# q of eight heads at a time by two 64-row PE tiles, with VectorE's steps queued by deadline

**Chip, cores, metric.** One core of one Trainium2 chip. The metric is device time in microseconds (us), the median of several executions of the whole program. PE is TensorE, ACT ScalarE, DVE VectorE, POOL GpSimd, SP SyncE.

## The reference, cut to what matters

```python
# S=2048 rows, D=576; 32 q heads, 16 k/v heads of 128; only the last W=512 keys are used
xn = layernorm(x)
q  = (xn @ wq)                      # 576 -> 32 heads x 128
p  = softmax(q @ k.T * Dh**-0.5)    # 512 keys, two q heads share one k/v head
s  = (p @ v) @ wo                   # 4096 -> 576
h  = gelu(layernorm(xn) @ w1)       # then rows shifted by -1, +1, -2, +2 per quarter
x1 = xn + shift(h) @ w2
g  = silu(x1 + gelu(layernorm(x1) @ w3) @ w4)
out = x + s * g
```

576 input rows are 4.5 chunks of the 128 rows that PE takes at once. That half chunk is what the change is about.

## The kernel before

Attention runs through 128 steps `u`: four blocks of 512 rows, 32 heads each. In a step PE makes the scores of a head (four matmuls of 512 columns, one ACT exp each), q of the next head (five matmuls) and the probabilities by v of the head before (16 matmuls of 129 columns). DVE divides by the row sum and writes a tile `o`, which a DMA transpose on the sync queue turns into `oT`. Matmuls of wo (block before), w1 and w2 are dealt out over the steps as filler. An MLP phase follows; it uses two 64-row tiles already.

```python
qT_pool = pool("qT_pool", 3)
o_pool = pool("o_pool", 4)          # four o tiles: four heads may wait for their transpose
...
def stage_q(u):
    qb, h = divmod(u, Hq)
    w = wq_b[(u // 4) % NWQ]
    hh = h % 4
    psq = ps_pq.tile([P, QB], FP32, name="psq", tag="pq")
    for kc in range(NDC):           # five chunks, the fifth half empty
        nc.tensor.matmul(psq[:, :], lhsT=w[:, kc, hh * Dh:(hh + 1) * Dh], rhs=xT_b[qb % 2][:, kc, :],
                         start=(kc == 0), stop=(kc == NDC - 1))
    ...                             # eviction to qT: DVE in block 0, ACT later
...
def stage_t(u):
    o = o_t.pop(u)
    oT = oT_pool.tile([P, TB, P], BF16, name="oT")
    last_t[0] = nc.sync.dma_start(out=oT[:], in_=o[:].rearrange("p a b -> p (a b)"), transpose=True)
...
at(2, lambda: late(pT_t[2][0][0:1, 0:1], load_w1))   # late: POOL waits for an exp, then issues the load
for i in range(8):
    at(4 + 3 * i, lambda i=i: late(pT_t[4 + 3 * i][0][0:1, 0:1], lambda: load_wo(i)))
...
for j in range(2, NB * 8):
    at(4 * (j - 1) - 1, lambda j=j: load_wq(j))      # wq for four heads at a time
...
for i in range(4):                                   # the main loop, one step u
    if u < U:
        stage_s(u, i)
    if i == 0:
        if u + 1 < U:
            stage_q(u + 1)                           # q follows the first score of every head
        for fn in fill.get(u, []):
            fn()
        continue
    if i < 3 and 0 <= u - 1 < U:
        stage_v(u - 1, 2 * (i - 1))
    for fn in cut[i - 1]:                            # filler, in thirds
        fn()
```

During the first 32 heads the POOL queue also loads nearly all of k, v, wo, w1 and the next x.

## Time and profile before

| | before |
|---|---|
| median of 3 runs | 851.1 us (850.77 to 858.88) |
| profiled span, mean granted clock | 847.5 us, 0.999 |
| first exp | 12.9 us |
| first exp to first exp, heads 0 to 31, 32 to 63, 64 to 95 | 103.1, 133.7, 134.3 us |
| heads 96 to 127, then to the MLP's first matmul | 137.4, 32.3 us |
| MLP | 293.7 us |

The phases are read from the trace's records of the exps and of the first MLP matmul. The first group of 32 is shorter because it carries no wo matmuls.

The prediction shows the page, the waits and one head. One view it did not use is that of the tile `oT`, the transposes of the attention output: duration of the issue (ns: min/median/max), who waited for the tile, and the time from issue to landing.

```profile
L395 SPq DMA_TRANSPOSE oT<-o x128: 1188/1192/2397, 18.4 to 523.9; - x128
  DVE o L387: 4.3, 2
DMA to landing us min/median/max: 2.4/3.2/9.8
```

DVE had twice waited, 4.3 us together, for an `o` tile to come free: the slowest transpose landed 9.8 us after its issue, and four tiles at one head per 2.88 us cover 11.5 us, of which filling a tile takes some. This queue was just long enough.

### The profile page before, as it was taken

The numbers are of one execution on the slowest core, as the hardware profiler recorded it, in microseconds if no ns is written. First come the engines' busy times: TensorE is split into PE (matmuls) and PEld (weight loads), VectorE is DVE, ScalarE is ACT, GpSimd is POOL, SyncE is SP. The second block draws the span as 40 slices with busy tenths as digits, with TensorE's granted clock in tenths as the row PEclk, the third lists the DMA queues.
The fourth block names the chain that finished last, engine by engine and source line by source line (L and its number), as shares of the span: only waits on it lengthen the run. The fifth ranks groups of instructions, "written<-read, shape, count | busy, mean of one in ns | idle before, by whom it ended". The sixth has DMA issues, their size and how long they took to land.

```text
span 847.5 us, 19375 instructions
## 1 busy us (share of the span) xinstructions
PE 826.8 (98%) x7896; PEld 485.0 (57%) x7980; DVE 427.7 (50%) x1351; ACT 460.9 (54%) x825; POOL 76.9 (9%) x134
## 2 busy tenths in 40 slices
PE   8999899999999999999999999999999999999996
PEld 5665555665564565565566565455555555555555
DVE  5778841267751166762154884052247537635324
ACT  5776763598793388784379874132333333334610
POOL 3441200310010111010001100000000000000000
PEclk9999999999999999999999999999999999999999
DMA  7996751473372174363048336992003301310101
GB/s 181 234 234 159 157 97 41 117 125 91 87 136 43 41 130 99 91 126 82 19 82 164 70 79 105 307 342 47 2 2 74 99 2 43 69 64 15 44 15 46
DMA packets 139983, 83.94 MB, mean 99 GB/s; under 512 B 106944, under 2 KB 133248, under 8 KB 139888
## 3 DMA queue, kind: packets, MB, share of 16 engines
q1 hardware_dynamic: 130048, 53.01, 30.6%
q0 software_dynamic: 8448, 28.15, 11.8%
q10 hardware_dynamic: 1392, 1.48, 0.5%
q8 instruction: 64, 1.05, 0.5%
q14 instruction: 31, 0.25, 0.1%
HBM read 49.17 MB, written 9.44 MB: 69 GB/s over the span
## 4 chain that ended last, share of the span: by engine, by line

## 5 line engine op out<-in xcount | busy, mean ns | idle before, releaser
L367 ACT ACTIVATE pT<-sc 128x512 bf16<-128x512 f32 x512 | 290.3, 596 | 103.5 <-PE sc L365 91.4
L365 PE MATMUL sc<-qT,kT 128*128 128x512 bf16 x493 | 175.1, 378 | 1.3 <-DVE qT L355 0.6
L382 PEld LDWEIGHTS <-pT 128*128 128x128 bf16 x2048 | 139.5, 98 | 52.9 <-DVE o L387 2.5
L382 PE MATMUL po<-v_sb,pT 128*128 128x129 bf16 x2048 | 161.4, 220 | 3.2 <-DVE o L387 2.0
L350 PE MATMUL psq<-xT_b,wq_b 128*128 128x512 bf16 x603 | 151.9, 379 | 2.5 <-DMA xT_b<-xn_b 0.4
L386 DVE RECIPROCAL ri_b<-po 128x2 f32<-128x2 f32 x256 | 43.0, 168 | 189.3 <-PE po L382 185.3
L731 PE MATMUL ph<-xT_b,w_s 64*128 64x512 bf16 x976 | 127.1, 376 | 2.3 <-DVE fence L721 2.1
L768 PE MATMUL pm<-w_s,h 64*128 64x512 bf16 x864 | 122.2, 377 | 0.9 <-DVE fence L721 0.9
L406 PE MATMUL pswo<-wo_sb,oT 128*128 128x512 bf16 x497 | 114.2, 379 | 0.8
L387 DVE TENSOR_TENSOR o<-po,ri_b 128x256 bf16<-128x256 f32 x256 | 107.9, 422 | 10.7 <-DMA oT<-o 4.3
L749 ACT ACTIVATE h<-ph 128x512 bf16<-128x512 f32 x67 | 39.4, 597 | 133.9 <-PE ph L731 133.9
L350 PEld LDWEIGHTS <-wq_b 128*128 128x128 bf16 x640 | 62.4, 98 | 74.4 <-issue 2.2
L768 PEld LDWEIGHTS <-h 64*128 64x128 bf16 x1728 | 70.8, 94 | 56.7 <-issue 1.6
L406 PEld LDWEIGHTS <-oT 128*128 128x128 bf16 x1024 | 64.9, 98 | 55.2
L768 PE MATMUL pr<-w_s,h 64*128 64x64 bf16 x864 | 90.2, 189 | 0.2 <-ACT h L749 0.2
L731 PEld LDWEIGHTS <-w_s 64*128 64x128 bf16 x1152 | 57.3, 94 | 51.0 <-issue 2.8
L357 ACT ACTIVATE qT<-psq 128x512 bf16<-128x512 f32 x96 | 57.4, 598 | 28.1 <-PE psq L350 26.7
L747 DVE COPY hx<-ph 128x512 f32<-128x512 f32 x55 | 38.0, 692 | 67.8 <-PE ph L731 67.8
L365 PEld LDWEIGHTS <-kT 128*128 128x128 bf16 x512 | 47.4, 97 | 28.4 <-DVE qT L355 1.2
L227 POOL DMA_DIRECT2D wq_b<-in_A_wq_dram x30 | 23.4, 780 | 314.4 <-PE psq L350 295.4
L721 DVE TENSOR_SCALAR fence<-ph,ph 1x1 f32<-1x1 f32 x61 | 12.6, 206 | 53.9 <-PE ph L731 53.4
L749 ACT ACTIVATE h<-hx 128x512 bf16<-128x512 f32 x55 | 34.6, 630 | 8.5 <-DVE hx L747 7.0
(114 smaller groups left out, 641.3 us busy)
## 6 DMA issues: line engine op xcount, KB each, us to landing
wq_b<-in_A_wq_dram POOLq DMA_DIRECT2D x30, 512.0 KB, 5.3
w_s<-in_B_w_dram SPq DMA_DIRECT2D x9, 576.0 KB, 7.0
wo_sb<-in_A_wo_dram POOLq DMA_DIRECT2D x8, 576.0 KB, 5.0
w_s<-in_B_w_dram SPq DMA_DIRECT2D x9, 512.0 KB, 7.9
x_dram<-x SPq DMA_DIRECT2D x4, 576.0 KB, 3.5
x<-x_dram SPq DMA_DIRECT2D x4, 576.0 KB, 5.1
s_b<-s_dram SPq DMA_DIRECT2D x4, 576.0 KB, 5.4
x_b<-in_A_x_dram SPq DMA_DIRECT2D x4, 576.0 KB, 6.6
```

What stands on the lines that cost most here:

```text
L350: nc.tensor.matmul(psq[:, :], lhsT=w[:, kc, hh * Dh:(hh + 1) * Dh], rhs=xT_b[qb % 2][:, kc, :], start=(kc == 0), stop=(kc == NDC - 1))
L357: nc.scalar.activation(out=qT[:, :], in_=psq[:, :], func=ACT.Copy)
L365: nc.tensor.matmul(sc[:, :], lhsT=kT[:, g, kc * P:(kc + 1) * P], rhs=qT_t[u][:, :], start=True, stop=True)
L367: nc.scalar.activation(out=pT[:, :], in_=sc[:, :], func=ACT.Exp, scale=SCALE)
L382: nc.tensor.matmul(po[:, j, :], lhsT=pTs[kc][:, tt * P:(tt + 1) * P], rhs=v_sb[:, g, kc, 0:Dh + 1], start=(kc == 0), stop=(kc == KCH - 1))
L386: nc.vector.reciprocal(out=ri, in_=po[:, :, Dh])
L387: nc.vector.tensor_tensor(out=o[:, t0:t0 + 2, :], in0=po[:, :, 0:Dh], in1=ri.unsqueeze(2).to_broadcast([P, 2, Dh]), op=ALU.mult)
L406: nc.tensor.matmul(ps, lhsT=oT_t[qb * Hq + h][:, tt, :], rhs=wo_sb[:, h, lo:hi], start=(h == 0), stop=(h == Hq - 1))
L731: nc.tensor.matmul(ps[i][:, :], lhsT=lhsT, rhs=xT[half, kc, :], start=first, stop=last, skip_group_check=True)
L747: nc.vector.tensor_copy(out=src[:, :], in_=ps[i][:, :])
L749: nc.scalar.activation(out=h3[:, :], in_=src[:, :], func=ACT.Gelu_apprx_tanh)
L768: nc.tensor.matmul(out, lhsT=h3_t[b, fc][half, tt * P:(tt + 1) * P], rhs=w4_s[fc // WS][half, fc % WS, lo:hi], start=key not in started, s ...
```

## The change

**Intent.** A half chunk of one head and a half chunk of another run side by side on two 64-row tiles of PE, so two heads take 9 slots in place of 10. As each change between 128-row and 64-row matmuls costs about 0.1 us (read from the trace in the prediction), q is made in blocks of eight heads. DVE and ACT get a fixed order, in which a small scheduler deals LN and gelu steps by deadline, against a credit that grows with PE's estimated time.

```diff
-        qT_pool = pool("qT_pool", 3)
-        o_pool = pool("o_pool", 4)
+        qT_pool = pool("qT_pool", 8)
+        o_pool = pool("o_pool", 5)
...
-            eng.dma_start(out=w[0:DR, NF, :], in_=A_wq[NF * P:D, c0:c0 + 4 * Dh])
+            for half in (LO, HI):                      # the tail of wq in both halves
+                eng.dma_start(out=w[half, NF, :], in_=A_wq[NF * P:D, c0:c0 + 4 * Dh])
...
-        def stage_q(u): ...
+        def stage_qs(u0, n):
+            unit(0.7)                                  # DVE: LN/gelu steps for up to 0.7 us
+            for u2 in range(u0, u0 + n, 4):
+                pairs = []
+                for u in (u2, u2 + 2):
+                    psp, tag = ((ps_pq, "pq"), (ps_po, "po"))[(u == u2) == (u0 > 0)]
+                    ps = [psp.tile([P, QB], FP32, name="psq", tag=tag) for _ in range(2)]
+                    q_half(xT, u, ps, [(kc, ((0, LO), (1, HI))) for kc in range(NDC)], True)
+                    f = small.tile([1, 1], FP32, name="fence")      # DVE reads both banks
+                    nc.vector.tensor_scalar(out=f[:, :], in0=ps[0][0:1, 0:1], scalar1=ps[1][0:1, 0:1],
+                                            scalar2=None, op0=ALU.add)
+                    unit(0.7)
+                    pairs.append((u, ps))
+                for u, ps in pairs:                    # then the halves swapped
+                    q_half(xT, u, ps, [(kc, ((1, LO), (0, HI))) for kc in range(NF)], False)
+                    ...
+                    nc.scalar.activation(out=qT_t[u][:, :], in_=ps[0][:, :], func=ACT.Copy)
+                    nc.vector.tensor_copy(out=qT_t[u + 1][:, :], in_=ps[1][:, :])
...
+        def pe(u, atoms, us=0.216):                    # filler, with its time for the credit
+            pe_fill.setdefault(u, []).extend((fn, us) for fn in atoms)
...
+                pe(u + 3, b2_rem(bb))                  # twenty 64-column matmuls, counted at 0.216
...
-        for j in range(2, NB * 8):
-            at(4 * (j - 1) - 1, lambda j=j: load_wq(j))
+        at(1, lambda: load_wq(2))
+        for j in range(3, NB * 8):                     # two at once
+            at(8 * (j // 2 - 1) + 1 + j % 2 if j > 3 else 4, lambda j=j: load_wq(j))
...
+                if u == 4:
+                    stage_qs(4, 4)
+                elif u % 8 == 0 and 0 < u < U:
+                    stage_qs(u, 8)
                 for i in range(4):
...
+                    v, tt = (u - 2, 2 + i) if i < 2 else (u - 1, i - 2)
+                    if 0 <= v < U:
+                        stage_v(v, tt)
+                    for fn, t in atoms[n * i // 4:n * (i + 1) // 4]:   # filler, in quarters
+                        fn()
+                    quarter(us)                        # credit for DVE steps
```

Filler tables, LN steps and buffers of x are moved to suit; the MLP gets finer LN steps.

## The prediction

> **What bounds the kernel now.** I read the page first: busy shares, then the slices.
>
> ```profile
> PE 826.8 (98%) x7896; PEld 485.0 (57%) x7980; DVE 427.7 (50%) x1351; ACT 460.9 (54%) x825; POOL 76.9 (9%) x134
> PE   8999899999999999999999999999999999999996
> ACT  5776763598793388784379874132333333334610
> PEclk9999999999999999999999999999999999999999
> ```
>
> TensorE (PE) is the candidate, at full clock. ScalarE (ACT) averages half, but its slices swing between 3 and 9: an average over stages with different limits. Attention, which the change touches, ends where the first matmul of the MLP starts, at 553.77 us (line below). The waits of PE inside 17 to 553.7 us:
>
> ```profile
> PE po L382 <- DVE o L387: 2.0, 1, 2.0
> PE psq L350 <- DMA xT_b<-xn_b: 0.4, 1, 0.4
> PE po L382 <- ACT pT L367: 0.3, 1, 0.3
> ```
>
> Only 2.7 us of 537. So PE itself bounds attention, and matmuls must be counted by start-to-start, not by their modelled durations. One plain head, from the timeline at 241.7 us (PE and ACT lines; L365 scores, L382 probabilities by v, L350 q, L367 exp, L357 the q eviction):
>
> ```profile
> 241.72 0.38 PE L365 MATMUL sc<-qT,kT 128*128 128x512 bf16 x1
> 241.92 0.60 ACT L357 ACTIVATE qT<-psq 128x512 bf16<-128x512 f32 x1 [0.21 <-PE psq L350]
> 241.94 0.63 PE L382 MATMUL po<-v_sb,pT 128*128 128x129 bf16 x8
> 242.41 0.38 PE L365 MATMUL sc<-qT,kT 128*128 128x512 bf16 x1
> 242.42 2.17 ACT L367 ACTIVATE pT<-sc 128x512 bf16<-128x512 f32 x4
> 242.62 0.63 PE L382 MATMUL po<-v_sb,pT 128*128 128x129 bf16 x8
> 243.09 0.59 PE L365 MATMUL sc<-qT,kT 128*128 128x512 bf16 x2
> 243.29 0.17 DVE L386 RECIPROCAL ri_b<-po 128x2 f32<-128x2 f32 x1
> 243.49 0.42 DVE L387 TENSOR_TENSOR o<-po,ri_b 128x256 bf16<-128x256 f32 x1
> 243.52 1.24 PE L350 MATMUL psq<-xT_b,wq_b 128*128 128x512 bf16 x5
> 244.60 0.38 PE L365 MATMUL sc<-qT,kT 128*128 128x512 bf16 x1
> ```
>
> The head takes 244.60 - 241.72 = 2.88 us. Five q matmuls take 244.60 - 243.52 = 1.08, so 0.2155 each; four scores 0.86; eight v matmuls 242.41 - 241.94 = 0.47, so 0.94 for sixteen, 0.0588 each. Sum 2.88: no gap. Over attention: 512 score, 640 q, 512 wo, 100 w1 and 80 w2 matmuls of 512 columns are 1844 x 0.2155 = 397; 2048 v by 0.0588 = 120; 592 of 64 columns at about 0.03 (81 wo remainders took 2.53 us) = 18; K transposes 3. That is 538 against 537 measured.
>
> Second reading: ACT. The q eviction starts at 241.92 and the next exp at 242.42, although its scores were ready before: 0.495 us per 128x512 tile back to back, less than the 0.596 duration. A head's four exps need 4 x 0.495 = 1.98 us, and with the eviction 2.47 of 2.88. PE hides that now.
>
> **What the Trainium skill says.** *TensorE: Matmul & The Clock Gate*, Part 1, "Wait - 56ns, not 53.3ns?": warm 512-column matmuls start 215.7 ns apart; the trace has 0.2155 us. *TensorEngine Tiling (Array Packing)*, "Key Properties": tiles work in parallel, but changing the tiling mode drains TensorE; and "Gotcha 1: PSUM Pressure": different row tiles must not access one PSUM bank at the same time, which is why each half pass is followed by a fence. *ScalarE: Activation LUTs*, "What ACT_TABLE_LOAD costs": 186 ns + 0.833 ns per column, overlapping by about 93 ns back to back, so an estimate of 0.52 us for 512 columns; the trace says 0.495, which I use.
>
> The MLP of this kernel already runs two 64-row tiles, so pairs and mode switches can be measured:
>
> ```profile
> 551.31 2.53 PE L406 MATMUL pswr<-wo_sb,oT 128*128 128x64 bf16 x81
> 553.77 1.04 PE L731 MATMUL ph<-xT_b,w_s 64*128 64x512 bf16 x8
> ...
> 574.92 1.04 PE L731 MATMUL ph<-xT_b,w_s 64*128 64x512 bf16 x8
> 575.78 0.40 PE L731 MATMUL ph<-xT_b,w3r_s 64*128 64x512 bf16 x2
> ...
> 804.45 1.04 PE L731 MATMUL ph<-xT_b,w_s 64*128 64x512 bf16 x8
> 805.42 1.58 PEld L931 LDWEIGHTS <-h 128*128 128x128 bf16 x14 [0.42 <-issue]
> ```
>
> Four pairs take 575.78 - 574.92 = 0.86, 0.215 a pair: two 64-row matmuls cost one slot. Switching back, the last pair started at about 805.10, so without a switch the next would start at 805.32; it starts at 805.43: 0.11 us. The switch in at 553.77 is also about 0.1 us late.
>
> **The change, part by part.**
>
> 1. *q.* 576 rows are 4.5 chunks of 128; before, a head takes 5 slots, the fifth half empty. Two heads by two tiles take 9 slots instead of 10. 64 pairs save 64 slots x 0.2155 = **-13.8 us**, all on PE. That is the whole direct gain, 1.6%.
>
> 2. *Mode switches.* q now comes in blocks: 4 heads at the start, 4 at head 4, then 8 at each of 15 places. 17 blocks x 2 x 0.11 = **+3.7 us**.
>
> 3. *Entry of a block.* After the first, a block's first pair writes the two po banks. One has just been filled by the v matmuls before it and must be evicted first. In the timeline the v group's last matmul starts at about 243.03 and VectorE (DVE) ends its multiplication at 243.91, while PE could go on at 243.09: 0.82 us. 16 entries would be 13.1 us. I have only the order in the source for it (another order moves the wait to the end of the block), so I take half: **+6.5 us**.
>
> 4. *Inside a block.* Eight heads are 36 slots, 7.76 us. DVE has four fences (0.2 each), four evictions (0.69 each) and up to five allowances of 0.7 for LN and gelu steps: 7.1 us. An allowance ahead of a fence or eviction that is due makes PE wait, chiefly where the second four heads want the banks of the first. Estimate 0.15 to 0.3 for each of 17: **+2 to 4 us**, taken as 2.5.
>
> 5. *Between blocks.* A head without q is 0.86 + 0.94 = 1.80 us of PE but 1.98 of ACT. **ACT becomes the bound of plain heads.** Three score banks let PE run ahead only about 1.5 us, so in a block of q ACT starves. Heads with wo (6.9 us each), w1 (1.08) or w2 (1.08) matmuls stay on PE: 0, 12, 9 and 13 of the four times 32 heads by the new table; in the first 32, 14 have K transposes of 0.24, which nearly balance it. So about 62 plain heads lose 0.18 = 11 us, less about 0.4 each time PE has built up a lead from a filled head (about ten times): 7. With the first quarter about 8; I take three quarters: **+6 us**.
>
> 6. *LN and gelu in DVE order.* They are moved, not removed. PE now loses only 2.7 us to waits in attention, one of 2.0 behind a q/k/v-side transfer; I credit **-2.5 us**.
>
> 7. *Start.* LN of the first tile writes 64 duplicate columns first (four of 0.29 us, overlapped, about +0.8), and four heads of q precede the first score instead of one, with ACT idle and then ACT-bound for two heads: about **+2 us**.
>
> 8. *MLP.* Same matmuls. PE waits there for late fences add up to 3 us; finer LN steps could recover **-1 us**.
>
> Sum: -13.8 + 3.7 + 6.5 + 2.5 + 6 - 2.5 + 2 - 1 = +3.4, so 854.5. The steps 3 and 5 are where I chose; whoever laid out the new queues so finely may have hidden more than I see, so I shade the result to **853 us**.
>
> **Rivals.** (a) *PE only:* all waits hidden, 1 and 2 and 6 alone: 851 - 13.8 + 3.7 - 2.5 = 838. For it: PE is 98% busy and waits for nobody today. Against: taking q from plain heads puts their PE time under the ACT time. (b) *A wait takes the place of the saved slots:* entry waits in full (13.1), ACT in full (8), banks 4: 851 - 13.8 + 3.7 + 13.1 + 4 + 8 - 2.5 + 2 - 1 = 864.5. For it: the eviction chain of 0.82 us is as large as the saving of an eight-head block, 4 x 0.2155 = 0.86. (c) *Transfers:* the LN output transposes share the sync queue with the o transposes (3.2 us median to landing), and wq is now loaded two blocks at once. If w1 waits for transposed LN output, some us three times: 860 or more. Against: the old waits on transfers are 0.4 us and one hidden 2.0.
>
> **Range and chances.** (a) and (b) bracket the case: 838 to 864.5; the range is **840 to 866**. Faster by over 2% means under 834, below even rival (a): 4%. Slower by over 2% means above 868, which needs (b) and (c) together: 8%. Within 2%: 88%.
>
> **What would show it.** Right: L350's successors are 1152 matmuls of 64 rows, pairs 0.215 apart, blocks about 7.8 us; ACT exps 0.495 apart in plain heads, with PE waiting for them; PE waits for DVE at block entries of 0.8. Step 3 is wrong if those entry waits are under 0.3; step 5 is wrong if plain heads run at 1.80 us. The prediction is wrong downward if both fail, upward if any one wait on a transfer exceeds 3 us or if DVE's queue is late by more than 0.5 us at most fences.

## The result

| | before | after |
|---|---|---|
| median of 4 runs of the same rounds | 851.0 us | 911.92 us (907.49 to 915.18) |
| ratio | | 1.0684 [1.0621, 1.0747] |
| profiled span, mean granted clock | 847.5, 0.999 | 913.3, 0.977 |
| first exp | 12.9 | 17.1 (+4.2) |
| heads 0 to 31 | 103.1 | 143.4 (+40.3) |
| heads 32 to 63 | 133.7 | 150.8 (+17.0) |
| heads 64 to 95 | 134.3 | 140.2 (+5.9) |
| heads 96 to 127, then to the MLP | 137.4, 32.3 | 139.6, 32.4 (+2.2) |
| MLP | 293.7 | 289.9 (-3.8) |

The rows don't hold the same q: by the order in the source, the changed kernel makes 13 more q slots of 0.2155 us before the first exp, 2 more in heads 0 to 31, and 16, 16 and 47 fewer in the three rows after. So the last row of attention, +2.2 us with 10 us of slots less, hides a loss too.

Ratios, here and below, are of fast runs alone, and not quite the ratio of the medians. Executions over 1.5% slower than the fastest of the same kernel are left out of the means. The change costs 7%: slower, and far outside the predicted range.

The page of the changed kernel, busy shares and slices (tenths of 1/40 of the span):

```profile
PE 849.0 (93%) x8492; PEld 492.3 (54%) x8492; DVE 475.9 (52%) x1463; ACT 432.1 (47%) x793; POOL 90.6 (10%) x161
PE   8864988999989999999999998999999999999997
PEclk9986989999999999999999999999999999999999
```

PE now has holes. The deep ones are in slices 3 and 4 (46 to 91 us), within the first 32 heads, and the granted clock falls in the same place. The waits of PE in those heads, 17 to 161 us (total us, times, longest us):

```profile
PE po L458 <- DVE o L465: 23.7, 4, 19.6
PE psq L433 <- DVE o L465: 6.9, 6, 4.5
PE psq L433 <- DMA wq_b<-in_A_wq_dram: 2.2, 1, 2.2
```

The same from 161 to 624 us, the rest of attention:

```profile
PE po L458 <- DVE o L465: 7.7, 7, 2.0
PE psq L433 <- DVE o L465: 5.4, 11, 1.1
PE psx L598 <- DVE x L609: 5.4, 11, 0.9
```

"DVE o L465" is the multiplication that empties the `po` bank. It was put down as the releaser, so the next question is what DVE itself waited for. The timeline at the longest wait; in brackets, how long the engine was idle and what ended it:

```profile
80.22 0.42 DVE L465 TENSOR_TENSOR o<-po,ri_b 128x256 bf16<-128x256 f32 x1 [20.14 <-DMA oT<-o]
80.70 0.61 PE L458 MATMUL po<-v_sb,pT 128*128 128x129 bf16 x4 [19.56 <-DVE o L465]
```

DVE stood 20.14 us because no `o` tile was free: all five were behind transposes that had not landed. The tile that came free first had been full at 51.89 us; its transpose was issued at 56.37, after LN transposes that stood before it on the sync queue, and landed at 80.13. So the order of the queue cost 4.5 us of that time, and the transfer 23.8. The tile view of `oT` after:

```profile
L475 SPq DMA_TRANSPOSE oT<-o x128: 1188/1192/7442, 22.0 to 594.6; - x128
  DVE o L465: 29.0, 5
DMA to landing us min/median/max: 2.4/2.6/24.7
```

The median is no worse than before; the maximum of a transpose's issue went from 2.4 to 7.44 us and that of its landing from 9.8 to 24.7. While the 7.44 us transpose ran (64.7 to 72.1 us), the DMA queues carried this (packets, MB, share of 16 engines):

```profile
q0 software_dynamic: 363, 1.30, 85.7%
q1 hardware_dynamic: 392, 0.09, 7.2%
```

q0 are POOL's weight loads, q1 the sync queue's transposes. Packet for packet the two queues got about the same number through; byte for byte the loads got fourteen times as much. The Trainium skill (*DMA: Bandwidth & Descriptors*, "Queues, rings and completion order") says that a DMA engine takes turns between the queues it has work for, a packet at a time. The counts agree with this, though from 72 to 76 us the transposes got about two packets for each one of the loads; no run isolates it.

What the hole does to the clock, by stretches of 10 us (busy us of PE, PEld, DVE, ACT and POOL, the clock, DMA share, GB/s), first before, then after:

```profile
70.00:80.00 10.00, 9.95 (x74) 5.63 (x73) 9.48 (x30) 7.39 (x14) 3.95 (x6) 1.00 0.71 170
```

```profile
70.00:80.00 10.00, 0.00 (x0) 0.00 (x0) 0.00 (x0) 0.00 (x0) 0.00 (x0) 0.50 1.19 183
80.00:90.00 10.00, 8.63 (x68) 5.68 (x70) 6.50 (x25) 5.06 (x9) 0.00 (x0) 0.73 0.56 72
```

With every compute engine idle the clock goes to 0.50, and when PE resumes it has 0.73 over the next 10 us: a stall is paid twice. The Trainium skill (*TensorE: Matmul & The Clock Gate*, Part 1, "What's actually happening") has it that the clock is halved after an idle window of about 3.4 us and comes back after a busy one; the trace agrees with the half. Its clock records have full clock again at 85.4 us, 4.7 us after PE resumed at 80.70.

Against this, a plain stretch shows that the two-tile q itself is as predicted:

```profile
417.93 0.39 PE L433 MATMUL psq<-xT_b,wq_b 64*128 64x512 bf16 x1
418.36 0.42 DVE L465 TENSOR_TENSOR o<-po,ri_b 128x256 bf16<-128x256 f32 x1
418.84 7.94 PE L433 MATMUL psq<-xT_b,wq_b 64*128 64x512 bf16 x71 [0.52 <-DVE o L465]
426.71 0.39 PE L441 MATMUL sc<-qT,kT 128*128 128x512 bf16 x1
```

The block's second matmul waits at the entry for the `po` bank to be emptied; the rest of it takes 426.71 - 418.84 = 7.87 us, 36 slots of 0.2155 and a switch.

### The profile page after: what moved, and what is told of

It reads as the page before. It is cut to its first block, busy times and chain, and to the rows that moved or that the text cites. A ratio compares the mean times of both kernels' runs of the same rounds, so it can differ in the third digit from the quotient of the medians.

```text
span 913.3 us, 20587 instructions
## 1 busy us (share of the span) xinstructions
PE 849.0 (93%) x8492; PEld 492.3 (54%) x8492; DVE 475.9 (52%) x1463; ACT 432.1 (47%) x793; POOL 90.6 (10%) x161
## 4 chain that ended last, share of the span: by engine, by line
## 5 line engine op out<-in xcount | busy, mean ns | idle before, releaser
L443 ACT ACTIVATE pT<-sc 128x512 bf16<-128x512 f32 x512 | 269.6, 683 | 121.8 <-PE sc L441 119.0
L458 PE MATMUL po<-v_sb,pT 128*128 128x129 bf16 x2048 | 205.4, 223 | 31.5 <-DVE o L465 31.4
L458 PEld LDWEIGHTS <-pT 128*128 128x128 bf16 x2048 | 159.5, 99 | 111.7 <-DVE o L465 36.9
L441 PE MATMUL sc<-qT,kT 128*128 128x512 bf16 x512 | 196.1, 384 | 1.5 <-ACT pT L443 1.3
L433 PE MATMUL psq<-xT_b,wq_b 64*128 64x512 bf16 x1152 | 139.3, 388 | 15.2 <-DVE o L465 12.3
L465 DVE TENSOR_TENSOR o<-po,ri_b 128x256 bf16<-128x256 f32 x256 | 108.6, 424 | 37.8 <-DMA oT<-o 29.0
L486 PE MATMUL pswo<-wo_sb,oT 128*128 128x512 bf16 x512 | 118.6, 379 | 0.5 <-ACT x L496 0.5
L433 PEld LDWEIGHTS <-wq_b 64*128 64x128 bf16 x1152 | 60.4, 96 | 88.2 <-DVE o L465 15.8
L425 ACT ACTIVATE qT<-psq 128x512 bf16<-128x512 f32 x64 | 38.2, 597 | 113.2 <-PE psq L433 113.2
L441 PEld LDWEIGHTS <-kT 128*128 128x128 bf16 x512 | 50.4, 99 | 20.9 <-issue 11.1
L426 DVE CAST qT<-psq 128x512 bf16<-128x512 f32 x64 | 44.1, 689 | 17.4 <-PE psq L433 16.7
```

What stands on the lines that cost most here:

```text
L425: nc.scalar.activation(out=qT_t[u][:, :], in_=ps[0][:, :], func=ACT.Copy)
L426: nc.vector.tensor_copy(out=qT_t[u + 1][:, :], in_=ps[1][:, :])
L433: nc.tensor.matmul(ps[k][:, :], lhsT=w[half, kc, hh * Dh:(hh + 1) * Dh], rhs=xT[half, kc, :], start=(first and kc == 0), stop=(not first a ...
L441: nc.tensor.matmul(sc[:, :], lhsT=kT[:, g, kc * P:(kc + 1) * P], rhs=qT_t[u][:, :], start=True, stop=True)
L443: nc.scalar.activation(out=pT[:, :], in_=sc[:, :], func=ACT.Exp, scale=SCALE)
L458: nc.tensor.matmul(po[:, j, :], lhsT=pTs[kc][:, tt * P:(tt + 1) * P], rhs=v_sb[:, g, kc, 0:Dh + 1], start=(kc == 0), stop=(kc == KCH - 1))
```

## The experiments

My theory: the loss needs two things together. q in blocks makes heads pass in bursts, about 2.0 us apart between blocks in place of an even 2.88, and each burst hands its transposes to DMA engines full of weight loads; with five `o` tiles, a landing over some 10 us then stops DVE and PE. A smaller second part comes from DVE's fixed order. Rival 1: the order of the sync queue, where LN transposes sit among those of `o`. Rival 2: the tile switches and fences. Each text in quotes was written before its run. All ten gave outputs within tolerance. The kernel before took 851.1 us in the median beside e1 to e6, 856.3 beside e7 to e10, and 852.3 beside e11 and e12. Across calls, compare ratios or lengths within a profile, not totals.

### Part of the loads away: e1_wo_eighth

```diff
-                nc.tensor.matmul(ps, lhsT=oT_t[qb * Hq + h][:, tt, :], rhs=wo_sb[:, h, lo:hi], ...
+                nc.tensor.matmul(ps, lhsT=oT_t[qb * Hq + h][:, tt, :], rhs=wo_sb[:, h % 4, lo:hi], ...
-        for i in range(8):
+        for i in range(1):
             at(4 + 3 * i, lambda i=i: late(pT_t[4 + 3 * i][0][0:1, 0:1], lambda: load_wo(i)))
```

One eighth of wo is loaded and used for all heads: wrong, though the difference stays within the tolerance.

> The changed kernel with one of the eight wo loads (4.1 of about 12 MB of loads of the first 32 heads are left out; every head then multiplies by the first four heads' rows of wo, a wrong result on purpose). Theory (the o transposes wait behind load packets): the waits of the first 32 heads, 33 us in the trace of the changed kernel, fall to under 12, the 20 us one is gone, total 880 to 892. Rival 1 (o transposes stand in the sync queue behind LN transposes that wait for VectorE's late steps): under 6 us less, above 905. Rival 2 (tile switches and block entries cost it): no change.

Measured: 896.32 and 889.94 us, ratio 1.0488 [1.0394, 1.0583]; heads 0 to 31 took 123.4 us in place of 143.4. PE's waits for `o` there, 17 to 141 us:

```profile
PE po L458 <- DVE o L465: 12.2, 3, 6.8
```

The 19.6 us stall is gone by taking away loads that PE does not need for another block. That the 12.2 us left are due to the other loads is not shown. The size was missed: with the smaller waits PE still waits 17.4 us there, of 33.9 in the changed kernel, where under 12 was expected; the total is just outside 880 to 892.

### q by head again, all else kept: e3_q_by_head

```diff
-        def stage_qs(u0, n): ...           # and q_half
+        def stage_q(u): ...                # five 128-row matmuls, as before
...
-        at(1, lambda: load_wq(2))
-        for j in range(3, NB * 8):
-            at(8 * (j // 2 - 1) + 1 + j % 2 if j > 3 else 4, lambda j=j: load_wq(j))
+        for j in range(2, NB * 8):
+            at(4 * (j - 1) - 1, lambda j=j: load_wq(j))
...
+                    if i == 0 and u + 1 < U:
+                        stage_q(u + 1)
...
+                    us += 1.08 if i == 0 and u + 1 < U else 0
```

> The changed kernel with q head by head in 128-row mode as before (five matmuls after each head's first score, one wq load per four heads); the LN and gelu queue, the memory layout and the order of v stay as changed. Theory (heads in bursts of 1.8 us produce o faster than the transposes can leave while loads run): the first 32 heads come back to 98 to 106 us, total 845 to 862. Rival 1 (the new queue order on its own): still above 885.

Measured: 853.32 us (profiled, clock 0.998) and 883.62 us (clock 0.982, slow, so there is no ratio). In the profiled run heads 0 to 31 took 102.0 us, and PE waited in 17 to 117 us only this:

```profile
PE psq L412 <- DMA wq_b<-in_A_wq_dram: 2.3, 1, 2.3
PE po L442 <- DVE o L449: 2.0, 2, 1.6
```

The order of DVE, of the sync queue and of the LN transposes is the changed kernel's; without bursts the large waits are gone in this run, so rival 1 is out as a sufficient cause. (e3 also loads wq once per four heads again, not two at once; no run separates that from the bursts, but e9 below loads it so too and keeps waits for `o`.) One transpose still took 4.79 us and one landed after 15.5, but five tiles at 2.88 us cover 14.4. The run at 883 shows that this version too is near an edge.

### Blocks without tiles: e4_no_tiles

```diff
-                    q_half(xT, u, ps, [(kc, ((0, LO), (1, HI))) for kc in range(NDC)], True)
-                    f = small.tile([1, 1], FP32, name="fence")
-                    ...
+                    for k in range(2):
+                        ps = psp.tile([P, QB], FP32, name="psq", tag=tag)
+                        for kc in range(NDC):        # 128 rows, no fence, same banks
+                            nc.tensor.matmul(ps[:, :], lhsT=w[:, kc, hh * Dh:(hh + 1) * Dh], rhs=xT[:, kc, :], ...
```

> The changed kernel, q in the same blocks of 4 and 8 heads over the same four banks, but in 128-row matmuls, five per head, with no half passes and no fences. Theory: 64 slots more (13.8 us), 34 switches at about 0.1 and the waits inside a block less (4 to 7 us), and the stalls behind transfers stay: 916 to 924. Rival 2 (tile switches and fences are the loss): falls below 890.

Measured: 908.32 and 906.76 us, ratio 1.0658 [1.0619, 1.0697], against 1.0684 of the full change: the same. Rival 2 is out, and the stalls stayed: PE waits 21.7 us for `o` in the first 32 heads. The total was missed: giving back the 13.8 us of slots should have made it slower, and did not. This is not only because slots are waited away behind transfers. From head 32 to the MLP, where neither profile has a transfer wait over 0.2 us, this run took 463.9 us and the changed kernel 462.9, although the q of heads 40 to 127 is made there, 44 of the 64 slots (9.5 us). A plain group of eight heads, one without filler, took 23.9 us here and 24.2 with the tiles. Over these heads the waits of q for `o` at the block entries fall from 5.4 us to 1.1, and there are no switches. In this order of work the tiles gained nothing even where no transfer is in the way.

### Loads issued when a q block begins: e6_loads_in_blocks

```diff
-        at(2, lambda: late(pT_t[2][0][0:1, 0:1], load_w1))
-        for i in range(8):
-            at(4 + 3 * i, lambda i=i: late(pT_t[4 + 3 * i][0][0:1, 0:1], lambda: load_wo(i)))
+        V, X, O, K = load_v, lambda i: load_x(i, nc.gpsimd), load_wo, load_k
+        for u, loads in {3: [(V, 2), (K, 2)], 7: [(V, 3), (X, 1), (V, 4), (O, 0)],
+                         15: [(V, 5), (K, 3), (O, 1), (O, 2), (O, 3)], 23: [(V, 6), (V, 7), (O, 4), (O, 5), (O, 6)],
+                         31: [(O, 7)]}.items():
+            ...                                   # (w1 with u == 3)
+            at(u, lambda u=u, some=some: late(pT_t[u][3][0:1, 0:1], some), 3)
```

The same bytes, but begun in the 7.8 us in which PE makes q and no new `o` tiles come. wq for later heads is likewise issued right at its block.

> The changed kernel with the loads of k, v, x, w1 and wo of the first 32 heads issued only when a block of q begins (gated on the last exp of the head before), same bytes, same sync queue order. Theory (transposes wait behind loads, and a block of q is time without o transposes): the waits of the first 32 heads fall from 33 us to 8 to 18, total 885 to 900. Rival 1 (sync queue order): unchanged, above 905.

Measured: 883.35 and 892.18 us, ratio 1.0425 [1.0299, 1.0552]; heads 0 to 31 took 111.6 us. PE's longest waits in 17 to 130 us:

```profile
PE ph L540 <- issue: 3.9, 1, 3.9
PE psq L433 <- DVE o L465: 2.8, 6, 0.7
```

The profile names no releaser for the first ("issue"); `ph` reads LN's transposed output. From some 33 us of waits to about 8 (with small ones not shown), as expected, with q in blocks, with tiles and with the same transposes. With e3 this is the case for "both together": undoing either removes the big stalls in the profiled run.

### The filler's cost in the credit: e7_rem_cost

```diff
-                pe(u + 3, b2_rem(bb))
+                pe(u + 3, b2_rem(bb), 0.029)
```

Twenty remainder matmuls of w2 were counted at 0.216 us each, and last 0.029. DVE was thus dealt LN steps for 4.3 us of PE time that were 0.6. In the changed kernel it looks like this, PE at the end waiting for the eviction behind them:

```profile
267.37 1.44 DVE L149 TENSOR_SCALAR xn_b<-xn_b,ln_mv,nr_y 128x64 bf16<-128x64 bf16 x4
268.73 0.16 DVE L464 RECIPROCAL ri_b<-po 128x2 f32<-128x2 f32 x1
269.41 0.29 PE L458 MATMUL po<-v_sb,pT 128*128 128x129 bf16 x2 [1.99 <-DVE o L465]
```

> The kernel with loads in blocks (e6_loads_in_blocks) and one number more: the 20 matmuls of 64 columns at the end of each w2 group are counted at 0.029 us for the VectorE step queue, not 0.216. With 0.216 the queue believes in 3.7 us of PE time that does not exist and puts up to 1.2 us of LN steps into each of four short quarters. Theory (VectorE's steps then stand ahead of the o evictions): the waits of v for o at those four places, 9.5 us in e6's trace, nearly go; 872 to 882. Rival (o held by transfers there too): no change, 883 to 892.

Measured on top of e6: 886.83 and 880.73 us, ratio 1.0316 [1.0237, 1.0395]. PE's waits for `o` from 161 to 560 us, e6 and then e7:

```profile
PE po L458 <- DVE o L465: 7.4, 7, 2.0
```

```profile
PE po L458 <- DVE o L465: 1.0, 2, 0.6
```

The mechanism is shown (6.4 us), and heads 32 to 63 took 144.9 us in place of 150.6. The total of 872 to 882 was missed in the median (883.8, one run of two within it): the profiled run had a wait of 6.6 us for `o` in the first heads (one transpose landed after 18.8 us), which hid it, and on this chip the kernel before was 5 us slower too.

### Entry, w2 bank and first gelu: e8_pq_first

```diff
-                    psp, tag = ((ps_pq, "pq"), (ps_po, "po"))[(u == u2) == (u0 > 0)]
+                    psp, tag = ((ps_pq, "pq"), (ps_po, "po"))[u > u2]
...
-                        stage_s(u, i)
+                        early = u % 8 == 0 or u == 4          # three scores right after a block
+                        for kc in ([0, 1, 2], [], [], [3])[i] if early else [i]:
+                            stage_s(u, kc)
...
-                    for fn, t in atoms[n * i // 4:n * (i + 1) // 4]:
+                    cut = (n * max(i - 1, 0) // 3, n * i // 3) if u in thirds else (n * i // 4, n * (i + 1) // 4)
+                    for fn, t in atoms[cut[0]:cut[1]]:        # w2 over the last three quarters
```

and the first two w1 groups two heads later.

> As e7_rem_cost, and: each q block writes the pq banks first and the po banks second, and after a block three scores go ahead of v; the w2 matmuls of a head are spread over its last three quarters instead of all four; the first two w1 groups come two heads later. Theory: the block entry waits (16 of 0.58 us) go without coming back at the end of the block, the eleven 0.6 us waits of w2 for its bank go, the 4 us wait for LN's transposes at the end of the first 32 heads goes: 20 us less than e7 together, 852 to 862. Rival (another wait takes their place): 864 or more.

Measured on top of e7: 865.57 us median (863.34 to 866.56), ratio 1.0094 [1.0042, 1.0147]. Waits at block entries went from 8.2 us in e7 to 0.3, those of w2 for its bank from 5.4 to none. Heads 32 to 63 took 139.9 us, 5.0 less. The range of 852 to 862 was slightly missed, and the rival's, 864 or more, was met: other waits took their place. Two in the first 32 heads remain, 5.2 us for `o` and 7.1 us of w1 for LN's output: its last transpose was issued at 95.27 us, the slowest of them landed 19.8 us after its issue, and the first w1 matmul starts at 115.2.

### Fours in place of eights: e9_fours

```diff
-                elif u % 8 == 0 and 0 < u < U:
-                    stage_qs(u, 8)
+                elif u % 4 == 0 and 4 < u < U:
+                    stage_qs(u, 4)
...
+        for j in range(2, NB * 8):
+            at(4 * (j - 2), lambda j=j: load_wq(j))
```

> As e8_pq_first but q in blocks of four heads throughout (32 blocks instead of 17). Theory (in runs of eight heads without q ScalarE's exps, 0.495 against PE's 0.45 a quarter, and o evictions fall behind; in runs of four the lead of three score banks covers it): 30 mode switches more cost 3 us, 6 to 10 us of waits go: 845 to 856. Rival (ScalarE is no bound; switches are dear): 4 to 8 us slower than e8.

Measured: 866.87 us median (863.36 to 869.09), ratio 1.0116 [1.0056, 1.0176], where 845 to 856 was expected. That is as e8, so the rival's 4 to 8 us more did not come either. A burst of four did not remove the waits for `o`: they were 8.4 us, 7.1 of them in the first 32 heads. A plain group of eight heads took 23.4 us, as in e8 (23.45): two more switches bought nothing.

### q by head with the order mended: e10_head_mended

```diff
-                pe(u + 3, b2_rem(bb))
+                    thirds.add(u + tt)
+                pe(u + 3, b2_rem(bb), 0.029)
...                                               # w2 over the last three quarters, as in e8
```

> As e3_q_by_head (q head by head, 128 rows, new LN and gelu queue), with the counted cost of the w2 remainders and the spread of w2 over three quarters as in e8. Theory: what the new queue gives without the blocks: 843 to 851 in runs where the transfers of the first 32 heads do not pile up (one of two runs of e3 was 30 us longer), so the mean may be higher. If e8 or e9 is not below this, the two-tile q has no gain here even mended.

Measured on top of e3: 853.37 us median (851.15 to 855.35), ratio 0.9952 [0.9900, 1.0004], above the 843 to 851 expected. So all of the change except blocks and tiles, with two small mendings, equals the kernel before within the interval.

### More o tiles, q by head: e11_head_o10

```diff
-        qT_pool = pool("qT_pool", 8)
+        qT_pool = pool("qT_pool", 3)
-        o_pool = pool("o_pool", 5)
+        o_pool = pool("o_pool", 10)
```

q by head needs only three qT tiles, and the room goes to `o`. (The changed kernel itself has no room for ten.)

> As e10_head_mended (q head by head) with the SBUF of five q tiles it does not need given to o: ten o tiles instead of five, three q tiles instead of eight. Theory (a slow o transpose stops PE only when all o tiles are waiting for theirs): the 6.5 us in which v waits for o fall below 2 and single long runs vanish; 0.985 to 0.993 of the kernel before. Rival (the transposes are slow on average, so more tiles only postpone the wait): waits stay, ratio 0.995 or more.

Measured: four fast runs of 845.59 to 850.12 us, ratio 0.9919 [0.9860, 0.9977]; and four slow ones of 863.13 to 873.33 at clocks of 0.987 to 0.991. With the slow ones the median is 856.63 us, against 852.33 of the kernel before. That the slow runs would vanish was wrong. The profiled run is a slow one, and its longest wait is for a load, not for `o`:

```profile
PE psq L412 <- DMA wq_b<-in_A_wq_dram: 14.5, 5, 7.1
PE po L442 <- DVE o L449: 6.2, 3, 5.6
```

More `o` tiles let transposes wait longer, but not wq arrive sooner. And the waits for `o` did not fall below 2 us in this run: with ten tiles they are still 6.2, and one transpose landed only after 27.2 us. There is no profile of a fast run. As half of its runs were slow, I don't call it a winner.

### More o tiles, fours: e12_fours_o9

```diff
-        qT_pool = pool("qT_pool", 8)
+        qT_pool = pool("qT_pool", 4)
-        o_pool = pool("o_pool", 5)
+        o_pool = pool("o_pool", 9)
```

> As e9_fours (two-tile q in blocks of four) with nine o tiles and four q tiles instead of five and eight. Theory: the 9 us of the first 32 heads behind o go to under 3; 0.995 to 1.005 of the kernel before. If it lands within 0.5% of e11, the 13.8 us of saved slots are all spent on switches and ScalarE's bound even without stalls; if it is 1% below e11, the two tiles pay once the stalls are gone.

Measured: 863.04 us median (853.99 to 864.45), ratio 1.0081 [1.0027, 1.0136]. The ratio is above the expected 0.995 to 1.005. In its profile (the run of 858.13 us, the second fastest), heads 0 to 31 took 102.6 us, one transpose still landed only after 19.3 us, and yet PE hardly waited for `o`: nine tiles at 23.4/8 = 2.9 us a head cover 26 us.

```profile
PE ph L540 <- issue: 2.9, 1, 2.9
PE po L458 <- DVE o L465: 1.6, 5, 0.5
```

This run is the two-tile q nearly free of stalls, and it is not faster than q by head (e11's fast runs, same chip and rounds). One reason stands in its timeline: between blocks ACT runs back to back, 16 exps in 7.94 us. In the trace's records each starts 0.478 us after the one before it (the 7.94 us take in the whole of the last), so four take 1.91 us, against 1.80 of PE.

```profile
348.85 7.94 ACT L443 ACTIVATE pT<-sc 128x512 bf16<-128x512 f32 x16
355.91 4.06 PE L433 MATMUL psq<-xT_b,wq_b 64*128 64x512 bf16 x36
359.91 0.82 PE L441 MATMUL sc<-qT,kT 128*128 128x512 bf16 x3
```

A plain group of eight heads is 23.4 us here and 23.0 in e11. By the trace's records, the 23.4 are 22.03 of matmul slots, 0.38 for four switches and 0.83 of waits for ACT, with a small rest. The saved slots are there, but ACT and the switches take them back. Outside heads 0 to 31 this profile is 8.7 us longer than e11's (753.7 against 745.1), 1.5 of them in the MLP; there the stalls of the first heads play no part.

The comparison by totals is weaker than it looks: "fast" leaves out e11's four runs over 860 us, while e12's four runs of 863 to 864 us count. Best against best it is 845.6 to 854.0, median of all runs 856.6 to 863.0; in each of them e12 is behind.

## Why the prediction was wrong

The predicted sum was 854.5, shaded to 853; 911.9 was measured. By its steps:

1. **q slots, -13.8: right.** Pairs start 0.215 us apart; a plain group of eight heads has 22.18 us of slots, where 8 x 2.88 would be 23.04.
2. **Switches, +3.7: right.** About 0.1 us each, 34 of them.
3. **Entries, +6.5: about right.** Leaving out the one wait of 4.5 us, `psq` waits for `o` sum to 2.4 us in the first 32 heads and 5.4 later: 7.8. e8 shows that another order of banks removes nearly all of it.
4. **Banks inside a block, +2.5:** about right, as far as the trace tells. A plain group of eight in the changed kernel takes 24.2 us. By start-to-start times these are 22.2 of slots, 0.2 of switches, 0.5 at the entry, some 0.2 more inside the block and 1.0 of waits for ACT.
5. **ACT-bound plain heads, +6: right in kind and sum.** By the trace's records, scores that follow a v group wait some 7 us in all. The parts were off: 0.495 us is the distance from a copy to an exp, exps start 0.478 apart, so a head needs 1.91 us of ACT, not 1.98. (And two w1 groups, at heads 27 and 29, do fall in the first 32 heads, where it counted none.)
6. **LN and gelu in DVE order, -2.5: this step failed, in sign and in size,** and with it the account of transfers: the sum has no term for `o` transposes at all. It said that PE "now loses only 2.7 us to waits in attention, one of 2.0 behind a q/k/v-side transfer", and so there was a little to gain. The old wait of 2.0 us was PE's share of DVE waiting for `o` tiles (4.3 us, twice): the sign of a transpose queue at its limit. In the changed kernel that queue costs PE most of 33 us in the first 32 heads. Beyond it, the new DVE order adds 7.7 us of waits for `o`, of which e7 shows 6.4 to be the miscounted filler, and 5.4 us of w2 waiting for its one bank, which e8 removes.
7. **Start, +2: about right.** The first exp comes 4.2 us later, but 2.8 of these are the 13 slots of q that only moved there.
8. **MLP, -1: too small,** -3.8 measured.

The same failure stood in **rival (c)**, which put the transfer risk on LN's transposes before w1, at "860 or more", and was then set aside because "the old waits on transfers are 0.4 us and one hidden 2.0". Low waits in an even rhythm say nothing about a burst. Five tiles at 2.0 us a head cover some 10 us, and the old profile's slowest landing, 9.8 us, filled that already. The chance of 8% for slower "needs (b) and (c) together"; waits on transfers alone were enough, though those of `o` and not of w1 as (c) had it. Its own sign of being wrong upward, one wait on a transfer over 3 us, came true with 20.14.

**Sum.** Spans differ by 65.8 us: heads 0 to 31 by 40.3, of which e6 took back 31.8 (143.4 to 111.6) and e3 all; heads 32 to 63 by 17.0, of which 3.2 are three w1 groups of the first block moved there (so heads 0 to 31 of all new kernels have that much less to do). Of the remainder e7 took back 5.7 (the filler's cost) and e8 5.0 (entries and the w2 bank); some lowered clock is in it (0.67 in 270 to 280 us). The clock after stalls is part of each of these sums and is not told apart.

**What is shown, and what is not.** Shown: the big stalls are DVE without an `o` tile behind slow transposes; they shrink in the profiled runs when heads don't come in bursts (e3), when loads start elsewhere (e6) or are fewer (e1), and nearly vanish with nine tiles and fours (e12); tiles and fences don't make them (e4). More `o` tiles alone are no cure that is shown: e11's slow run waited with ten. Not shown: that turns by packet are the reason why a transpose is slow, and why the loads themselves were slow in these stretches (180 GB/s while nothing but DMA was running). Also open is why runs of one kernel on one chip differ by 2 to 4% (e3, e11). And of the 12.7 us between the means of e12's and e11's fast runs the profiles place 8.7 outside heads 0 to 31; the rest is open, and partly a matter of which runs count as fast.

## What to carry to other kernels

Before work is gathered into blocks, look at every queue that the even rhythm fed: compare tiles times the new, shortest interval with the *slowest* landing in the old trace, not with the median or the old waits. A small old wait for a buffer can be the sign of a full queue, and not only a small cost. And slots saved on one engine are worth only the distance to the next bound: here 2.88 us of PE against 2.47 of ACT per head became 1.80 against 1.91, so that, with switches and entry waits on top, 13.8 us of fewer slots bought no time even where nothing stalled.

## What the Trainium skill lacked or had wrong

- *TensorEngine Tiling (Array Packing)*, "Key Properties": says that a change of mode drains PE, but not what it costs. Here it was about 0.1 us (0.11 in the MLP before, 0.095 around e12's blocks).
- *ScalarE: Activation LUTs*, "What ACT_TABLE_LOAD costs": its figures give an estimate of 0.52 us for 512 columns back to back; measured 0.478 between exps, and 0.494 from a copy to an exp.
- *DMA: Bandwidth & Descriptors*, "Queues, rings and completion order": says that queues take turns by packet, but not what this does to a transpose's small packets beside large loads: 392 packets carried 0.09 MB while 363 of the loads carried 1.30 MB, and the issue of a transpose, 1.19 us in the median, took up to 7.44 us, 8.89 in e9.
